# A list scheduler gets measured durations, and bursts on TensorE must wait for its instruction packets

## The chip, the cores and the metric

The kernel runs on one core of a Trainium2 chip. The metric is the time of one execution on the device in microseconds (us). Five engines work side by side on a core, each through its own list of instructions in order: TensorE (PE, with its weight loads shown apart as PEld), VectorE (DVE), ScalarE (ACT), GpSimd (POOL) and SyncE (SP), which issues the DMA transfers. They meet only at semaphores.

## The reference, cut to what matters

Three stages follow each other on 4 x 768 = 3072 tokens of width 384:

```python
# attention with a decaying state, 8 heads of 48, for every step t:
y[t]  = r[t] @ (state + outer(u * k[t], v[t]))
state = w[t][:, None] * state + outer(k[t], v[t])
# first feed-forward, 384 -> 1536 -> 384
x = (sigmoid(x @ w_gate) * (x @ w_val)) @ w_out
# second feed-forward, 384 -> 2048 -> 384
h = x @ w_in
out = (h * tanh(softplus(h))) @ w_out2
```

All of it is float32.

## The kernel before, in words

**Tiling.** The 768 steps are cut into 24 chunks of 32, and two chunks make a pair: 12 pairs, numbered p = 0 to 11. A pair's 256 tokens go through attention and then, while the next pair's attention is under way, through the first feed-forward. The second feed-forward takes 512 tokens at a time once all pairs are through. A float32 matrix product is made of three float16 products (high by high, high by low, low by high), and the weights of all feed-forwards are decoded from 64-bit words into those halves on the chip, on ACT, DVE and POOL, until some 114 us (the first feed-forward's) and mostly from some 486 us on (the second's).

**Attention of a pair.** `fine(p)` multiplies and sums small blocks (POOL, DVE), `coarse(p)` turns operands on DVE, makes the scores on TensorE (`scores`, tile lp) and merges them (`merge`, tile X). `turn_keys` (pair 1 alone, tile kt) or `keys` bring the keys into place, `states_apart` (pairs 0 and 1) or `states` update the state (tile kp), and `rows_out` makes the output rows (tile yp). `turn` brings these rows into xt, through TensorE (tile xp) for pairs 0 and 1 and by a transposing DMA for the later ones.

**First feed-forward of a pair.** `gate(p, i)` makes 128 x 256 blocks of both products (tile gv). One call of its `fill` is nine matmuls with nine weight loads, 18 instructions; 24 fills belong to a pair. `out1` (tile o of the line L1201) is of the same size and shape. For these the weights have to be decoded, and for `gate` xt has to be there.

**Bursts.** The attention's matmuls are small and follow each other fast: lp, kt, kp and yp are one task each, of 129 to 385 instructions. They are called bursts and carry `burst=space(p)`: after one, no other burst is begun for 3.0 (pairs 0 and 1) or 5.0 planned us.

**Order.** Nothing is ordered by hand. Every piece of work is a `Task` with a planned cost on each engine that may do it, what it reads and writes, a `lat` (time after its end until others see it) and `words`, the number of its instructions on TensorE. `Plan.run` works out a due time for each (`late`), backward from the end. `Plan.schedule` then plays the plan forward in its own time: at each moment every free engine takes, of the tasks that are ready, the one with the earliest due time, on the engine where it is cheaper if two may do it. The order in which tasks are taken is the order in which each engine's instructions are written, so the planned costs decide the order and have no other effect: nothing on the chip waits for a planned time. While both DVE and POOL are busy with tasks that use the memory port they share (`port`), the plan lets them run at the shares in `SHARE` (L68). `COLD` = 1.9 (L37) is a factor on the cost of some early TensorE tasks, `BURST` = 1.42 that of a usual burst.

**Packets.** The plan takes TensorE's instructions to come in packets of `WORDS` = 256, with an offset of `ORIGIN` = 67, and counts them in `at_word`. `crowded` (L149) puts a burst of 208 words or more behind all other ready tasks if more than 208 of them lie within one packet. A burst that is put behind is still begun when TensorE has nothing else ready in the plan.

Of the kernel before, what the change touches and what calls it, by code (L numbers as in the profile page):

```python
# [48 lines left out]
COLD = 1.9  # L49
BURST = 1.42  # L50
# [2 lines left out]
TURNED = (1,)  # L53
KBANKS = ((('pg', 0), ('pg', 1)), (('at', 0), ('at', 2)))
ONE = 13
JOIN = 0.3
GATHER = 0.36
PARTS = ((), (0,), (1,), (2, 3))
SPACE = 3.0
# [3 lines left out]
WORDS = 256  # L63
MERGE = lambda p, e: e == 0
CROWD = 208
SWEEPS = 1
INF = float("inf")
SHARE = {"dve": 0.42, "pool": 0.72}  # L68
ENGS = ("pool", "dve")
W1HI = {"act": 0.83}  # L70
W1LO = {"dve": 0.92, "pool": 1.65}
# [11 lines left out]
class Plan:  # L83
# [57 lines left out]
            t.fn(e)  # L141

    def schedule(self, follow):
        now = rested = 0.0
        at_word = ORIGIN
        coming, busy, queues, order = [], {}, {}, []
        left = {t: len(t.deps) for t in self.tasks}

        def crowded(t):  # L149
            if t.words < CROWD:  # L150
                return False
            first = WORDS - at_word % WORDS
            return max(min(first, t.words), t.words - first) > CROWD

        def arrive(t):
            at = max([d.end + d.lat for d in t.deps], default=0.0)
            heapq.heappush(coming, (at, t.rank, t))

        def finish(t):
            t.end = now  # L160
            for n in follow[t]:
                left[n] -= 1
                if left[n] == 0:
                    arrive(n)

        def best(e):
            return min(
                (bool(t.burst) and (now < rested or crowded(t)), t.late, t.rank, t)
                for t in queues[e]
            )[1:]  # L170

        for t in self.tasks:
            if not t.deps:
                arrive(t)
        while len(order) < len(self.tasks) or busy:
            while True:
                while coming and coming[0][0] <= now + 1e-9:
                    t = heapq.heappop(coming)[2]
                    for e in t.cost:
                        queues.setdefault(e, []).append(t)  # L180
                picks = []
                for e in queues:
                    if queues[e] and e not in busy:
                        late, rank, t = best(e)
                        picks.append((late, rank, t.cost[e], e, t))
                if not picks:
                    break
                _, _, _, e, t = min(picks, key=lambda x: x[:3])
                for k in t.cost:
                    queues[k].remove(t)  # L190
                t.begin = now
                order.append((e, t))
                if e == "pe":
                    at_word += t.words
                if e == "none":
                    finish(t)
                else:
                    busy[e] = [t.cost[e], t]
                if t.burst:
                    rested = now + t.cost[e] + t.burst  # L200
            shared = all(e in busy and busy[e][1].port for e in SHARE)
            rate = {e: SHARE[e] if shared and e in SHARE else 1.0 for e in busy}
            step = min((busy[e][0] / rate[e] for e in busy), default=INF)
            if coming:
                step = min(step, coming[0][0] - now)
            now += step
            for e in list(busy):
                busy[e][0] -= step * rate[e]
                if busy[e][0] < 1e-9:
                    finish(busy.pop(e)[1])  # L210
        return order
# [3 lines left out]
def mixer_moe_kernel(  # L215
# [15 lines left out]
    add = plan.add  # L231
# [21 lines left out]
    A = fp.tile([128, 1184], F32, name="A")  # L253
# [6 lines left out]
    def attn(eng, cost, fn, reads=(), writes=(), lat=SEM, burst=0.0, words=18, port=False):  # L260
        add(eng, cost, fn, [*reads, "attention"], writes, lat, burst, words, port)

    def space(p):
        return SPACE if p < 2 else SPACED
# [25 lines left out]
    words = {}  # L290
# [38 lines left out]
    def decode(key, dst, n, count, slot, reads, high_on, lo_on, halves=False, blocks=None):  # L329

        raw = ("raw", slot)
        word = ("word", count % 2)
        low = ("low", count % 2)
        name = f"{key[0]}{key[1]}"

        def rebase(e):
            words[key] = dp.tile(
                [128, *n], F32, tag=f"word{count % 2}", name=f"word_{name}"  # L340
            )
            rebased(words[key], raws[key][:, :, :, 1])

        def bits3(e):
            lows[key] = dp.tile([128, *n], U32, tag=f"low{count % 2}", name=f"low_{name}")
            spare_bits(key)

        def join(e):
            bits = words[key].bitcast(U32)
            nc.vector.scalar_tensor_tensor(  # L350
                out=bits,
                in0=bits,
                scalar=3,
                in1=lows.pop(key),
                op0=ALU.logical_shift_left,
                op1=ALU.bitwise_or,
            )

        def high(e):
            put = nc.scalar.copy if e == "act" else nc.vector.tensor_copy  # L360
            put(out=dst()[:, 0], in_=words[key])

        def rest(e):
            engines[e].tensor_tensor(  # L364
                out=dst()[:, 1], in0=words.pop(key), in1=dst()[:, 0], op=ALU.subtract
            )

        add("act", 0.78, rebase, [raw, "consts", "table1"], [word])
        add("act", 1.1, bits3, [raw, "consts"], [low])
        add("dve", 0.85, join, [low], [word], port=True)  # L370
        if halves:
            combine(key, dst, word, low, reads, high_on, lo_on, count)
            return
        made = [[(key[0], f, a) for f in blocks or [key[1]]] for a in range(2)]
        add(high_on, 0, high, [word, *reads], made[0])
        add(lo_on, 0, rest, [word, *made[0]], made[1])
# [40 lines left out]
    def decode_early(name, i, dst, src, count):  # L417

        slot = count % 3
        raw = ("raw", slot)  # L420
        low = ("low", count % 2)
# [4 lines left out]
            lows[key] = dp.tile([128, KC, 256], U32, tag=f"low{count % 2}", name=f"low_{name}{i}")  # L426
            spare_bits(key)

        add("act", 1.1, bits3, [raw, "consts"], [low])
        for h in range(2):  # L430
            f = 2 * i + h
            hs = slice(128 * h, 128 * h + 128)
# [28 lines left out]
                    op=ALU.subtract,  # L461
                )

            add("act", 0.43, rebase, [raw, "table1"], [bank])
            add("dve", 0.48, join, [low], [bank])
            add("act", 0.39, high, [bank], [(name, f, 0)])
            add("dve", 0.47, rest, [bank, (name, f, 0)], [(name, f, 1)])

# [33 lines left out]
    def load_pair(p):  # L504
        edges = (0, C * DH, C * (DH + DP), BLK)

        def new(e):
            blk[p] = fp.tile([128, BLK], F32, tag=f"blk{p % 2}", name=f"blk{p}")

        def go(e, i):  # L510
            if i is None:
                new(e)
            cs = slice(0, BLK) if i is None else slice(edges[i], edges[i + 1])
            nc.sync.dma_start(out=blk[p][:, cs], in_=rkw[p, :, cs])

        keys = [("blk", p % 2, i) for i in range(3)]
        if p == 1:
            attn("sp", 3.6, lambda e: go(e, None), [], keys, lat=2.0)
            return

        after = [[], [("x2d", p - 4, KC - 1)], [("x2d", p - 3, 0)]]
        attn("none", 0, new, [], keys, lat=0.0)
        for i in range(3):
            late[p, i] = lambda i=i: attn(
                "sp", 1.2, lambda e: go(e, i), after[i] if p > 3 else [], [keys[i]], lat=2.0
            )
            if p <= 3 or i == 0:
                late.pop((p, i))()
# [19 lines left out]
    def fine(p):  # L548
# [3 lines left out]
        def products(mult, cost, shape, cell, scaled=False):  # L552
# [19 lines left out]
            if scaled:  # L572
                attn("dve", 0.95, times_u, ["U"], [pt], port=True)
            cells.append(("A", len(cells)))
            attn("dve", 0.86 if cost > 1 else 0.47, total, [pt, "A"], [cells[-1]])

        products(
            lambda e, pv, r, k: times(e, pv, r, k),
# [63 lines left out]
    def coarse(p, cells):  # L642
# [83 lines left out]
        attn(both, 0, lambda e: scaled(e, 5, 6, 1, 4), [WD], [(*RD, 2)])  # L726
        attn({"dve": 0.6, "pool": 1.05}, 0, lambda e: scaled(e, 2, 4, 2, 2), [WD, (*RD, 2)], [(*RD, 1)])
        parts = [(*RD, n) for n in range(3)]
        attn("pe", BURST, scores, [*parts, KD], [*banks, ("lp", p)], burst=space(p), words=256)
        attn("dve", 1.9, flip_a, [*cells], X[0] + X[1])  # L730
        for e in range(2):
            for n in range(4):
# [212 lines left out]
    def states_apart(p, e):  # L945
# [27 lines left out]
            for hf in range(2):  # L973
                decay(p, e, hf)
        parts = [("KK", p % 2, q, g, h) for q in range(4) for g in range(2) for h in range(2)]
        attn("pe", 1.17 * COLD, sums, [*parts, ("v", j % 3)], banks, burst=space(p), words=129)
        for hf in range(2):
            both = {"dve": 0.48} if j else {"act": 0.5, "dve": 0.48}
            attn(both, 0, lambda on, hf=hf: put(on, hf), [banks[hf]], S(j + 1)[2 * hf : 2 * hf + 2])
# [1 line left out]
    def rows_out(p, es, banks):  # L981
# [36 lines left out]
                                    stop=(n == 1 or j == 0),  # L1018
                                )

        cost = 2.58 if len(es) > 1 else BURST * (COLD if p < 2 else 1.0)
        attn("pe", cost, sums, [*X, *RD, *V, *old], banks, burst=space(p), words=257 if p else 193)
        xs = [[("xs", e, t, i) for i in range(2) for e in es] for t in range(2)]

# [91 lines left out]
    def gate(p, i):  # L1116
# [55 lines left out]

        def fill(o, h):
            w = [(("wg", "wv")[o], two[h], a) for a in range(2)]
            cold = COLD if p == 0 and two[h] < 3 else 1.0
            add("pe", 0.99 * cold, lambda e: sums(o, h), [*x, *w, "gates"], [banks[o]])

        def finish():
# [521 lines left out]
```

## Time and profile before

| | |
|---|---|
| time, median of 3 runs | 920.1 us (919.99 to 920.99) |
| span of the profiled execution | 917.8 us |
| what lies around the span | 2.3 us of the median |
| TensorE busy in the span | 866.2 us, 94% |
| VectorE, ScalarE, GpSimd busy | 633.6, 490.7, 506.4 us |
| instruction packets | queue q8: 102, 1.67 MB |

The profile is of one execution. A busy share is of the whole span, and stages with different limits lie in it, so the span is read stretch by stretch. Matmuls overlap, so the time of one is longer than the distance to the next. "Idle before" is time in which an engine stood still just before an instruction, with what ended it; "issue" there is time in which the engine waited for nothing that the profile shows. The granted clock of TensorE (PEclk) is 1.00 at 2.4 GHz and 0.50 at 1.2 GHz.

### The profile page before, as it was taken

How to read it: one execution, taken by the hardware profiler on the slowest of the kernel's cores; microseconds unless marked ns; L12 is line 12 of the kernel's file. 1: busy time of each engine (PE TensorE's matmuls, PEld its weight loads, DVE VectorE, ACT ScalarE, POOL GpSimd, SP SyncE). 2: the span in 40 equal slices, each digit the busy share in tenths (PEclk: the TensorE clock that was granted, in tenths of full speed). 3: DMA queues.
4: the chain of work that ended last, by engine and by line, in shares of the span. 5: the costliest groups of instructions: out<-in, count | busy, mean ns of one | idle time of the engine just before them, and what ended most of it. 6: DMA issues, size and time to landing. Idle time of an engine off the chain costs nothing.

```text
span 917.8 us, 29861 instructions
## 1 busy us (share of the span) xinstructions
PE 866.2 (94%) x13064; PEld 701.3 (76%) x13064; DVE 633.6 (69%) x1098; ACT 490.7 (53%) x1125; POOL 506.4 (55%) x562
## 2 busy tenths in 40 slices
PE   0578899999999999999999999999999999999998
PEld 0456788888888888888888885577677676776788
DVE  7897898877585777767688768765655655556541
ACT  2687854363543525262548777764655655556540
POOL 7996976646557474847553476543533434335320
PEclk9998999999999999999999999999999999999999
DMA  9277633222322232332306910100101002000001
GB/s 333 88 240 250 226 102 101 69 71 71 99 84 60 80 87 75 69 91 54 79 23 189 260 47 13 43 5 10 61 1 46 25 1 70 1 27 10 2 35 36
DMA packets 55315, 74.29 MB, mean 81 GB/s; under 512 B 19600, under 2 KB 36496, under 8 KB 55056
## 3 DMA queue, kind: packets, MB, share of 16 engines
q1 hardware_dynamic: 55184, 72.38, 26.3%
q8 instruction: 102, 1.67, 0.8%
q14 instruction: 29, 0.24, 0.1%
HBM read 58.99 MB, written 9.44 MB: 75 GB/s over the span
## 4 chain that ended last, share of the span: by engine, by line
PE 85%; POOL 4%; DVE 4%; ACT 3%; DMA 2%; issue 1%; SPq 0%; DVEq 0%; ACTq 0%; POOLq 0%
PE gv L1133 27%; PE h L1311 20%; PE o L1426 18%; PE o L1201 14%; PE yp L1013 3%; POOL pt L546 2%; PE kp L910 2%; POOL blk L546 1%; ACT KK L851 1%; ACT X L716 1%; PE lp L695 1%; POOL wos L364 1%; DMA raw_wv<-wv 1%; DVE A L566 1%; PE kt L806 0%
## 5 line engine op out<-in xcount | busy, mean ns | idle before, releaser
L1311 PE MATMUL h<-x,wis 128*128 128x512 f16 x864 | 199.9, 379 | 0.0
L1345 POOL TENSOR_TENSOR sum<-e 128x256 f32<-128x256 f32 x96 | 71.9, 748 | 179.9 <-ACT e L1322 179.9
L1133 PE MATMUL gv<-xt,wgs 128*128 128x256 f16 x1296 | 166.5, 274 | 4.8 <-DVE gt L1164 3.1
L1133 PE MATMUL gv<-xt,wvs 128*128 128x256 f16 x1296 | 165.6, 275 | 2.1 <-ACT sig L1144 1.8
L1201 PE MATMUL o<-gt,wos 128*128 128x256 f16 x1296 | 163.5, 273 | 0.0
L1311 PEld LDWEIGHTS <-wis 128*128 128x128 f16 x864 | 83.5, 98 | 82.9
L1133 PEld LDWEIGHTS <-wgs 128*128 128x128 f16 x1296 | 125.5, 98 | 21.7 <-issue 4.7
L1133 PEld LDWEIGHTS <-wvs 128*128 128x128 f16 x1296 | 126.4, 99 | 19.3 <-issue 2.2
L546 POOL TENSOR_TENSOR blk<-blk 128x384 f32<-128x384 f32 (+4 forms) x151 | 123.2, 829 | 30.1 <-DMA blk<-rkw 11.9
L1201 PEld LDWEIGHTS <-wos 128*128 128x128 f16 x1296 | 125.8, 98 | 17.9 <-issue 0.2
L546 POOL TENSOR_TENSOR pt<-blk 128x384 f32<-128x384 f32 x93 | 105.6, 1160 | 35.8 <-DMA blk<-rkw 33.1
L1322 ACT ACTIVATE e<-h 128x512 f32<-128x512 f32 x96 | 57.3, 597 | 85.9 <-PE h L1311 84.9
L1149 DVE SCALAR_TENSOR_TENSOR gv<-gv,sig 128x512 f32<-128x512 f32 x72 | 50.6, 703 | 54.2 <-ACT sig L1144 26.2
L1144 ACT ACTIVATE sig<-gv 128x512 f32<-128x512 f32 x72 | 42.1, 596 | 81.8 <-PE gv L1133 81.5
L1161 ACT CAST gt<-gv 128x512 f16<-128x512 f32 x72 | 42.2, 585 | 67.7 <-DVE gv L1149 67.5
L1426 PE MATMUL o<-wps,gt 128*128 128x192 f16 x612 | 74.0, 246 | 0.0
L887 POOL TENSOR_TENSOR s<-s,WD 128x384 f32<-128x384 f32 x40 | 37.1, 936 | 55.6 <-DVE s L939 35.7
L851 ACT COPY KK<-KT 32x192 f32<-32x192 f32 (+1 forms) x168 | 59.9, 357 | 10.9 <-DVE KT L836 8.5
L1364 DVE SCALAR_TENSOR_TENSOR gt<-e,gt 128x256 f16<-128x256 f32 x41 | 27.5, 683 | 49.6 <-ACT gt L1359 49.6
L1426 PE MATMUL o<-wps,wgs 128*128 128x192 f16 x498 | 59.4, 246 | 0.0
L1164 DVE TENSOR_TENSOR gt<-gv,gt 128x512 f16<-128x512 f32 x72 | 49.3, 685 | 13.2 <-ACT gt L1161 12.9
L1426 PE MATMUL o<-wps,wos 128*128 128x192 f16 x456 | 57.1, 246 | 0.0
(123 smaller groups left out, 1461.8 us busy)
## 6 DMA issues: line engine op xcount, KB each, us to landing
v<-vt SPq DMA_DIRECT2D x24, 480.0 KB, 4.1
blk<-rkw SPq DMA_DIRECT2D x22, 384.0 KB, 3.6
raw_wi<-wi SPq DMA_DIRECT2D x8, 768.0 KB, 5.7
raw_wp<-wo SPq DMA_DIRECT2D x8, 768.0 KB, 5.6
blk<-rkw SPq DMA_DIRECT2D x11, 512.0 KB, 4.3
raw_wg<-wg SPq DMA_DIRECT2D x6, 768.0 KB, 5.4
raw_wv<-wv SPq DMA_DIRECT2D x6, 768.0 KB, 5.4
raw_wo<-wo SPq DMA_DIRECT2D x6, 768.0 KB, 5.2
```

The costliest lines, as they stand in the source:

```text
L546: engines[e].tensor_tensor(out=pv, in0=a, in1=b, op=ALU.mult)
L851: nc.scalar.copy(out=to, in_=own)
L1133: nc.tensor.matmul(gps[p, i, o][:, h], w[:, a, kc, fs], xt[p][:, c, kc, :], start=(n == 0), stop=(n == 3 * KC - 1),)
L1144: nc.scalar.activation(out=sgs[p, i], in_=gps[p, i, 0], func=AF.Sigmoid, scale=1.0 / (SW * SX))
L1149: nc.vector.scalar_tensor_tensor(out=gps[p, i, 1], in0=gps[p, i, 1], scalar=SG / (SW * SX), in1=sgs.pop((p, i)), op0=ALU.mult, op1=ALU.mult,)
L1161: nc.scalar.copy(out=gt[p][:, 0, 2 * i : 2 * i + 2], in_=gps[p, i, 1])
L1164: nc.vector.tensor_tensor(out=gt[p][:, 1, 2 * i : 2 * i + 2], in0=gps[p, i, 1], in1=gt[p][:, 0, 2 * i : 2 * i + 2], op=ALU.subtract,)
L1201: nc.tensor.matmul(ops[p, c][:, :NT], wos[:, a, f, cs], gt[p][:, g, f, :], start=(f == 0 and n == 0), stop=(f == NF1 - 1 and n == 2),)
L1311: nc.tensor.matmul(hps[r, f], w2["wi"][:, a, kc, fs], x2[r][:, c, kc, :], start=(n == 0), stop=(n == 3 * KC - 1),)
L1322: nc.scalar.activation(out=es[r, f], in_=hps[r, f], func=AF.Mish, scale=ih)
L1345: engines[e].tensor_tensor(out=sums[0][:, n - 1], in0=a(), in1=b(), op=op)
L1426: nc.tensor.matmul(ops2[h, first], home(slots[r, i, name])[:, c, tsl], w2["wp"][:, a, w, i, :], start=(new and n == 0), stop=(n == 3 * NF2 ...
```

## The change

Two things are changed, both in the plan. No instruction is added or taken away; tasks are the same, and so are their dependencies.

**Durations.** Planned costs of decoding steps, sums, merges of the state, four early TensorE tasks, the shares of DVE and POOL and one transfer latency get other values.

**A condition for bursts.** When a task on TensorE reaches the end of a packet, the plan notes `ready`: the moment at which the end is reached plus `FETCH` = 3.2. A burst that would reach the next end before `ready`, by its planned cost, counts as unfit, as crowded bursts and those within the spacing do. The rest of the diff in `schedule` is the same selection with heaps in place of a scan.

```diff
-JOIN = 0.3
+JOIN = 0.32
+FETCH = 3.2
-SHARE = {"dve": 0.42, "pool": 0.72}
+SHARE = {"dve": 0.58, "pool": 0.78}
...
-        def crowded(t):
-            if t.words < CROWD:
-                return False
+        def unfit(t):
+            if now < rested:
+                return True
             first = WORDS - at_word % WORDS
-            return max(min(first, t.words), t.words - first) > CROWD
+            if t.words > first and now + t.cost["pe"] * first / t.words < ready:
+                return True
+            return t.words >= CROWD and max(min(first, t.words), t.words - first) > CROWD
...
         def best(e):
-            return min(
-                (bool(t.burst) and (now < rested or crowded(t)), t.late, t.rank, t)
-                for t in queues[e]
-            )[1:]
+            queue, bursts = queues[e]
+            while queue and queue[0][2] in taken:
+                pop(queue)
+            if not bursts:
+                return queue[0] if queue else None
+            found = min((unfit(t), late, rank, t) for late, rank, t in bursts)
+            if queue:
+                found = min(found, (False, *queue[0]))
+            return found[1:]
...
                 if e == "pe":
+                    first = WORDS - at_word % WORDS
+                    if t.words >= first:
+                        ready = now + t.cost[e] * first / t.words + FETCH
                     at_word += t.words
...
-        add("act", 0.78, rebase, [raw, "consts", "table1"], [word])
-        add("act", 1.1, bits3, [raw, "consts"], [low])
-        add("dve", 0.85, join, [low], [word], port=True)
+        add("act", 0.91, rebase, [raw, "consts", "table1"], [word])
+        add("act", 1.0, bits3, [raw, "consts"], [low])
+        add("dve", 0.96, join, [low], [word], port=True)
-        add("act", 1.1, bits3, [raw, "consts"], [low])
+        add("act", 1.0, bits3, [raw, "consts"], [low])
-            add("act", 0.43, rebase, [raw, "table1"], [bank])
-            add("dve", 0.48, join, [low], [bank])
-            add("act", 0.39, high, [bank], [(name, f, 0)])
-            add("dve", 0.47, rest, [bank, (name, f, 0)], [(name, f, 1)])
+            add("act", 0.5, rebase, [raw, "table1"], [bank])
+            add("dve", 0.52, join, [low], [bank])
+            add("act", 0.46, high, [bank], [(name, f, 0)])
+            add("dve", 0.51, rest, [bank, (name, f, 0)], [(name, f, 1)])
...
-                "sp", 1.2, lambda e: go(e, i), after[i] if p > 3 else [], [keys[i]], lat=2.0
+                "sp",
+                1.2,
+                lambda e: go(e, i),
+                after[i] if p > 3 else [],
+                [keys[i]],
+                lat=2.0 if p else 3.2,
...
-            attn("dve", 0.86 if cost > 1 else 0.47, total, [pt, "A"], [cells[-1]])
+            attn("dve", 0.9 if cost > 1 else 0.5, total, [pt, "A"], [cells[-1]])
...
-        attn("pe", BURST, scores, [*parts, KD], [*banks, ("lp", p)], burst=space(p), words=256)
+        attn("pe", BURST if p else 1.75, scores, [*parts, KD], [*banks, ("lp", p)], burst=space(p), words=256)
...
-        attn("pe", 1.17 * COLD, sums, [*parts, ("v", j % 3)], banks, burst=space(p), words=129)
+        attn("pe", 1.17 * (1.0 if j else COLD), sums, [*parts, ("v", j % 3)], banks, burst=space(p), words=129)
...
-        cost = 2.58 if len(es) > 1 else BURST * (COLD if p < 2 else 1.0)
+        cost = (2.58 if p else 3.4) if len(es) > 1 else BURST * (COLD if p < 2 else 1.0)
...
-            cold = COLD if p == 0 and two[h] < 3 else 1.0
+            cold = COLD if p == 0 and two[h] < 1 else 1.0
```

## Rows read from the trace of the kernel before

**Rows 1.** The page, TensorE's busy time over the whole span.
```profile
PE 866.2 (94%) x13064; PEld 701.3 (76%) x13064; DVE 633.6 (69%) x1098; ACT 490.7 (53%) x1125; POOL 506.4 (55%) x562
```

**Rows 2.** Busy time by stretch: stretch and length, PE, PEld, DVE, ACT, POOL, PEclk, DMA.
```profile
0.00:25.60 25.60, 0.00 (x0) 0.00 (x0) 17.72 (x22) 5.19 (x7) 18.82 (x26) 1.00 0.87 314
25.60:43.80 18.20, 11.34 (x460) 9.02 (x460) 16.34 (x24) 12.15 (x29) 17.81 (x17) 1.00 0.23 75
43.80:66.10 22.30, 18.87 (x319) 15.00 (x318) 22.30 (x33) 18.97 (x35) 20.57 (x20) 1.00 0.73 234
66.10:98.70 32.60, 23.41 (x682) 19.42 (x680) 26.54 (x46) 26.08 (x47) 23.25 (x22) 0.90 0.67 234
98.70:149.70 51.00, 47.78 (x1006) 41.71 (x1005) 45.61 (x69) 28.12 (x61) 39.96 (x36) 1.00 0.50 148
150.00:550.00 400.00, 399.92 (x7616) 354.60 (x7615) 294.57 (x505) 201.27 (x486) 236.22 (x250) 1.00 0.33 89
550.00:914.00 364.00, 364.00 (x2983) 260.90 (x2982) 209.82 (x404) 198.75 (x464) 149.75 (x195) 1.00 0.07 23
```

**Rows 3.** Waits of PE: who waited for whom, us in total, times, longest.
```profile
PE xp L1065 <- DVE xs L1044: 3.8, 2, 2.2
PE yp L1013 <- issue: 3.2, 1, 3.2
...
...
PE gv L1133 <- DMA xt<-xs: 1.4, 1, 1.4
```

**Rows 4.** PE in order of time, around pair 1's bursts: start, length, work.
```profile
69.19 4.51 PE L806 MATMUL kt<-first,blk 128*32 128x32 f32 x192 [2.82 <-ACT X L716]
...
75.61 1.15 PE L1133 MATMUL gv<-xt,wvs 128*128 128x256 f16 x9
76.69 0.31 PE L1013 MATMUL yp<-v,X 64*32 64x48 f32 x15
...
81.18 0.29 PE L1013 MATMUL yp<-s,RD 64*32 64x48 f32 x9 [3.20 <-issue]
...
82.72 3.47 PE L1133 MATMUL gv<-xt,wvs 128*128 128x256 f16 x18
...
98.66 1.16 PE L1133 MATMUL gv<-xt,wgs 128*128 128x256 f16 x9
```

**Rows 5.** PE in order of time, the same fills later.
```profile
115.40 2.13 PE L1133 MATMUL gv<-xt,wvs 128*128 128x256 f16 x18
```

**Rows 6.** Busy time and counts up to and within the stop in yp, columns as in Rows 2.
```profile
0.00:75.60 75.60, 36.89 (x988) 30.20 (x989) 64.56 (x91) 45.57 (x90) 66.62 (x68) 0.98 0.61 208
0.00:79.00 79.00, 39.27 (x1116) 32.17 (x1117) 67.73 (x100) 48.09 (x94) 69.94 (x72) 0.98 0.63 216
77.90:81.10 3.20, 0.08 (x9) 0.00 (x0) 2.75 (x4) 1.36 (x2) 3.12 (x5) 1.00 1.04 412
82.10:85.40 3.30, 3.30 (x18) 2.38 (x16) 1.46 (x4) 3.25 (x6) 0.00 (x0) 0.50 0.61 195
```

**Rows 7.** DMA queues: packets, MB, share of 16 engines.
```profile
q8 instruction: 102, 1.67, 0.8%
```

**Rows 8.** DVE in order of time, its wait for pair 1's xp.
```profile
86.57 0.56 DVE L1071 COPY xt<-xp 128x768 f16<-128x768 f16 x1 [3.01 <-PE xp L1065]
```

**Rows 9.** Groups of instructions by line and shape: busy us, mean ns, idle before.
```profile
L306 ACT ACTIVATE word_wv<-raw_wv 128x768 f32<-128x768 f32 x6 | 5.6, 941 | 0.0
```

**Rows 10.** DVE in order of time, the join of a tile beside busy and idle POOL.
```profile
35.38 1.79 DVE L350 SCALAR_TENSOR_TENSOR word_wv<-word_wv,low_wv 128x768 uint32<-128x768 uint32 x1
...
87.04 0.95 DVE L350 SCALAR_TENSOR_TENSOR word_wv<-word_wv,low_wv 128x768 uint32<-128x768 uint32 x1
```

**Rows 11.** POOL in order of time, its idle stretch and the state's decay.
```profile
88.93 1.65 POOL L364 TENSOR_TENSOR wvs<-word_wv,wvs 128x768 f16<-128x768 f32 x1 [7.00 <-ACT wvs L361]
91.94 0.83 POOL L887 TENSOR_TENSOR s<-s,WD 128x384 f32<-128x384 f32 x1 [1.36 <-DVE s L967]
...
94.34 1.54 POOL L887 TENSOR_TENSOR s<-s,WD 128x384 f32<-128x384 f32 x1
```

More of the change, by code (lines that the diff above doesn't have):

```diff
@@ L143, in schedule @@
     def schedule(self, follow):
-        now = rested = 0.0
+        now = rested = ready = 0.0
         at_word = ORIGIN
@@ L147, in schedule @@
         left = {t: len(t.deps) for t in self.tasks}
-        def crowded(t):
-            if t.words < CROWD:
-                return False
+        taken = set()
+        push, pop = heapq.heappush, heapq.heappop
+        def unfit(t):
+            if now < rested:
+                return True
             first = WORDS - at_word % WORDS
-            return max(min(first, t.words), t.words - first) > CROWD
+            if t.words > first and now + t.cost["pe"] * first / t.words < ready:
+                return True
+            return t.words >= CROWD and max(min(first, t.words), t.words - first) > CROWD
         def arrive(t):
             at = max([d.end + d.lat for d in t.deps], default=0.0)
-            heapq.heappush(coming, (at, t.rank, t))
+            push(coming, (at, t.rank, t))
         def finish(t):
@@ L177, in schedule @@
                 while coming and coming[0][0] <= now + 1e-9:
-                    t = heapq.heappop(coming)[2]
+                    t = pop(coming)[2]
                     for e in t.cost:
-                        queues.setdefault(e, []).append(t)
+                        queue, bursts = queues.setdefault(e, ([], []))
+                        if t.burst:
+                            bursts.append((t.late, t.rank, t))
+                        else:
+                            push(queue, (t.late, t.rank, t))
                 picks = []
                 for e in queues:
-                    if queues[e] and e not in busy:
-                        late, rank, t = best(e)
-                        picks.append((late, rank, t.cost[e], e, t))
+                    if e not in busy:
+                        found = best(e)
+                        if found:
+                            late, rank, t = found
+                            picks.append((late, rank, t.cost[e], e, t))
                 if not picks:
@@ L188, in schedule @@
                 _, _, _, e, t = min(picks, key=lambda x: x[:3])
-                for k in t.cost:
-                    queues[k].remove(t)
+                taken.add(t)
+                if t.burst:
+                    queues[e][1].remove((t.late, t.rank, t))
                 t.begin = now
```

## The prediction, made before the changed kernel ran

> **What bounds the kernel now.** I read four views: the page's busy times, busy time by stretch, TensorE's waits, TensorE's list in time. On the page TensorE is busy 866.2 of 917.8 us [rows 1], so 51.6 us are idle. The stretches say where: none of them lies late. From 150 to 550 us TensorE is busy 399.92 of 400.00, from 550 to 914 all of 364.00 [rows 2]. In these stretches a new order can only exchange work with work, at no gain. The idle time is before 149.7 us: 25.6 us until the first matmul, then 18.20 - 11.34 = 6.9, 22.30 - 18.87 = 3.4, 32.60 - 23.41 = 9.2 and 51.00 - 47.78 = 3.2 [rows 2], 22.7 in sum. Whatever the change does to the time, it does there: by the moment at which TensorE gets into its full stretch.
>
> What ends the waits there? Between 43.8 and 66.1 us DVE is busy 22.30 of 22.30 us [rows 2]: TensorE waits for vector work that nothing can hurry. From 66.1 to 98.7 all three vector engines have room: DVE 6.1, ACT 6.5, POOL 9.3 us [rows 2]. This is the stretch to look at. It ends with pair 1's first gv at 98.66 [rows 4], and TensorE's only other work in it, pair 0's fills, is short: 24 fills at 2.13 / 2 = 1.07 each [rows 5] are some 26 us, from 43.8 on. So fills are padding here, and the chain that counts is pair 1's attention: lp, kt, yp, kp, yp, kp, and through xp to xt.
>
> In that chain stand a 2.82 us wait of kt for ACT's merges, and a stop of 3.20 us in the middle of a yp burst, ended by "issue", with no semaphore named (both in [rows 4]). The counts explain it. TensorE has 13064 matmuls and as many loads [rows 1], 26128 instructions in the 102 transfers of queue q8 [rows 7], 256 each. With the plan's offset of 67 the packets end at 189 + 256 n. At 79.00 us, in the stop, 1116 + 1117 = 2233 have begun; 189 + 8 x 256 = 2237 [rows 6]. The packet before ended at 1981, and 988 + 989 = 1977 had begun at 75.60 [rows 6]. So TensorE crossed one end at about 75.6, needed the next packet at about 77.9, and went on at 81.18, 5.6 us after the crossing [rows 4]. In the stop the DMA engines are full: share 1.04, 412 GB/s [rows 6]. I take the packet to stand behind the loads of weights and of the next blocks; the rows show both at once, not the cause.
>
> The stop has a second price. From 82.10 to 85.40 the granted clock is 0.50, 1.2 GHz [rows 6], after TensorE had stood still; 18 gv matmuls take 3.47 us there and 2.13 at full clock [rows 4, 5], 1.3 more. And others wait behind: DVE 3.01 us for xp, POOL 7.00 for a cast [rows 8, 11].
>
> The Trainium skill, "Runtime: NRT & Kernel Launch", section "Instruction fetch mechanics", has blocks of 256 instructions, fetched by the sequencer while it runs the one before, at a cost it calls "mostly hidden", since instructions are dispatched more slowly than blocks arrive. By that the condition on bursts has nothing to save. The block size agrees with the counts above; on the cost this trace agrees for nearly all of the 102 packets, and differs by 3.20 us at one.
>
> **The change, part by part.** No instruction is added or removed, and all waits are the same dependencies; only places in each engine's list move. So no engine's busy time changes, except by the clock and by who runs beside whom.
>
> *The condition on bursts.* What it can save is the stop and the slow clock, 3.20 + 1.34 = 4.5 us. Would it catch this burst? If the order up to there stayed, hardly. The plan prices yp of pair 1 at 1.42 x 1.9 = 2.70 for 257 instructions; the burst began at about instruction 1995 (2233 less 119 matmuls and their loads), 242 before the end, so the plan has it reach that end 2.54 after its begin. It began about 1.0 after the crossing [rows 4, 6]; crossing plus 3.2 is 2.2 after the begin, and 2.54 is later. The condition lets it pass, by 0.3. On the chip the burst gets there in 1.2, and the packet came 4.6 after the begin. Moreover only the first end in a task is noted, and kt with its 385 instructions can cross two. So the condition helps only together with the shifted order: one or two fills fewer or more between kt and yp move the end out of the burst or the crossing away from it. Of the 256 possible offsets I count those as bad in which a crossing in or after kt is followed by another in yp within 5.6 us: with 384 + 54 + 256 = 694 instructions from kt to the end of yp, about 180 of 256, but those with the first crossing early in kt cost little, as 4 to 5 us pass. A stop over 1.5 us, with the first crossing 128 to 182 into kt, comes in 54 of 256, a fifth. Being put behind costs too, as the bursts are the chain: a fill is 1.07 [rows 5], one or two fills 1.5. Net 4.5 - 1.5 = 3.0 where the stop goes.
>
> *Durations of ACT and DVE.* The plan had rebase at 0.78, the trace has 0.941 [rows 9]; the new 0.91 is close. The join of a tile takes 0.95 beside an idle POOL and 1.79 beside a busy one [rows 10], a share of 0.53: the old plan had 0.85 / 0.42 = 2.02 there, the new one 0.96 / 0.58 = 1.66. POOL's share moves away from the trace: its decay takes 0.83 alone and 1.54 beside DVE's join [rows 11], 0.54, and the plan goes from 0.72 to 0.78. No row tells what order follows. The bounds: at best the new order uses the room of DVE in the two stretches after 66.1, 6.1 + 5.4 us [rows 2], of which the stop holds about 3 already, so some 8 gained; at worst it opens waits of the size of those for xp and of kt again, 3.8 + 2.8 [rows 3, 4], some 6 lost. I take 0, with a good half of the chance on the better side, since two of three are nearer to the rows.
>
> *TensorE's early costs* (cold factors off four fills and three kp bursts, 1.75 and 3.4 for pair 0) and *pair 0's latency*. TensorE is not the limit until 43.8, as DVE and POOL are busy 17.7 and 18.8 of the first 25.6 us and 16.3 and 17.8 of the next 18.2 [rows 2]. I take 0, with 2 us either way from the first 25.6, where the order of DVE and POOL can move.
>
> *After 150 us.* The condition puts bursts some fills later, and TensorE has fills enough: 0. If that cover went, it would show as idle time in the stretch of 399.92.
>
> **The sum.** 917.8 - 3.0 = 914.8 us of span; with the 2.3 us around it, 920.1 - 917.8, the forecast is 917.1 us.
>
> **The rivals.**
>
> *The gain is taken back at xt of pair 2, or the stop stays.* Pair 2's fills begin only after its xt, where TensorE now waits 1.4 us for the transfer [rows 3], ending at about 149.6. For it speaks that DVE is busy 45.61 of 51.00 us before it [rows 2]: if pair 2's chain is not earlier, 3.0 us saved at 98.7 are 3.0 us more wait there. The same time results if the burst passes the condition as worked out above. Against it: DVE's and POOL's idle 3.01 and 7.00 us behind the stop would shrink too. Time: 920.1, within 1 us. This time has two ways to it, the second of them small: that packets are on time in any order, and the stop in yp had another cause, such as the full DMA engines of [rows 6] holding up something that the trace does not show. Then the condition saves none of its 3.20 us, and only puts bursts behind. Its chance is 0.04 of the 0.25 below, as the stop falls within four instructions of a packet's end. The Trainium skill, "Runtime: NRT & Kernel Launch", section "Instruction fetch mechanics", has this rule.
>
> *Slower: the condition holds up pair 1's chain.* Six bursts stand between 62.5 and 98.7 us in a row, each may be put behind by up to 3.2 planned us, and fills are taken in their place, of which there is no lack until pair 0's are used up. It decides from two bursts put behind by two fills where no stop is saved: 2 x 2 x 1.07 = 4.3 us, less what overlaps with vector work: +4, 924. For it speaks that fills are padding up to 98.66; against, that most of these bursts wait for ACT or DVE anyway.
>
> *More: the new durations also take away kt's wait.* With merges and casts better placed on ACT, kt's 2.8 [rows 4] and half of xp's 3.8 [rows 3] go too: 3.0 + 2.8 + 1.9, about -8, 912.
>
> **How the numbers follow.** The forecast's case (-3, from -6 to -1) has 0.43, the gain of 8 has 0.10, no change 0.25, slower 0.22. Under 0.2%, 1.8 us, cannot be told from no change. Faster: 0.9 of the first, all of the second and little of the third, 0.50. Same: 0.26; slower: 0.24. The range leaves out a tenth at each side: 910 to 924.5; the likeliest case alone has 914 to 919.
>
> **What would show it.** Right: no "issue" wait over 1 us in yp or kp, a clock of 1.00 from 75 to 98 us, pair 1's first gv at about 95.5, and 150 to 550 us still full. Taken back: that gv earlier, but a longer wait for xt of pair 2. Wrong: a stop of 3 us at another packet's end, or pair 1's first gv after 100.

## The result, and the profile after

The changed kernel takes 924.39 us (median of 4 runs, 921.72 to 927.38) where the kernel before takes 920.05 in the same comparison: a ratio of 1.0055, 95% interval 1.0039 to 1.0071. It is slower by some 4 us; 3.0 us of gain were forecast. The profiled execution has a span of 919.9 us, the shortest of the four, 2.1 us longer than that of the kernel before; its rows show less of the loss than the medians do.

The page's row of TensorE and the busy time by stretch, of the changed kernel (columns as in [rows 2]):

```profile
PE 867.8 (94%) x13064; PEld 701.8 (76%) x13064; DVE 633.6 (69%) x1098; ACT 489.5 (53%) x1124; POOL 506.7 (55%) x563
```

```profile
25.60:43.80 18.20, 12.45 (x469) 9.97 (x470) 16.45 (x30) 15.57 (x36) 17.81 (x16) 1.00 0.34 110
43.80:66.10 22.30, 19.42 (x329) 15.49 (x327) 21.27 (x29) 17.41 (x32) 19.62 (x19) 1.00 0.78 266
66.10:98.70 32.60, 24.24 (x692) 20.54 (x692) 28.09 (x47) 27.13 (x48) 30.94 (x28) 0.90 0.68 228
98.70:149.70 51.00, 47.49 (x1000) 41.33 (x998) 46.39 (x73) 27.60 (x69) 38.53 (x36) 1.00 0.51 143
150.00:550.00 400.00, 397.27 (x7575) 351.13 (x7573) 293.37 (x498) 196.33 (x471) 232.58 (x248) 1.00 0.32 87
550.00:914.00 364.00, 364.00 (x2978) 260.63 (x2976) 208.02 (x401) 200.10 (x464) 148.29 (x194) 1.00 0.07 23
```

Against [rows 2], TensorE is busier in each of the first three stretches shown, by 1.1, 0.6 and 0.8 us. In the stretch from 150 to 550, which was full (399.92), it now stands still for 2.73 us. TensorE's waits in the same profile, to be read against [rows 3]:

```profile
PE kp L935 <- ACT KK L876: 2.5, 7, 0.4
PE gv L1158 <- DMA xt<-xs: 2.4, 2, 1.7
...
PE yp L1038 <- issue: 2.2, 2, 1.2
...
PE gv L1158 <- DVE X L741: 2.0, 1, 2.0
```

Two kinds of these reach into the late part. The gates wait for xt twice (1.7 us at pair 2, just before 150 us, and 0.7 at pair 3), and kp waits seven times for key copies on ACT, five of these times after 150 us, 1.85 us in sum. TensorE's list around pair 1's bursts, which answers to [rows 4]:

```profile
68.25 4.60 PE L831 MATMUL kt<-first,blk 128*32 128x32 f32 x192 [2.11 <-ACT X L741]
74.88 1.14 PE L1158 MATMUL gv<-xt,wgs 128*128 128x256 f16 x9 [2.03 <-DVE X L741]
...
81.12 0.23 PE L1038 MATMUL yp<-s,RD 64*32 64x48 f32 x2 [1.17 <-issue]
...
90.23 0.31 PE L1038 MATMUL yp<-s,RD 64*32 64x48 f32 x14 [1.08 <-issue]
...
93.73 2.30 PE L1226 MATMUL o<-gt,wos 128*128 128x256 f16 x9
...
97.37 1.16 PE L1158 MATMUL gv<-xt,wgs 128*128 128x256 f16 x9
```

Pair 1's first gv comes at 97.37, 1.29 us earlier, and 18 matmuls of out1, two fills or about 2 us, are done before it, where the kernel before had none: TensorE is 3.3 us further. I counted TensorE's matmuls of both traces in order, weighed by their kind, and compared the times at equal work. The changed kernel leads by 3.3 us between 128 and 141 us, by 2.6 once pair 2's gate runs, by 1.5 from 188 us on; it is level at 279, 1.3 behind at 363 and 2.1 behind from 547 us on. The early gain is there, and 5.4 us are lost later. Idle time is only part of that: of the 4.7 us lost after 150 us it holds 2.7, as a burst that is broken up also takes longer while TensorE counts as busy.

The steps of that loss are kp bursts and gate starts. Pair 7's kp, and the key copies on ACT before it, in the changed kernel (the kernel before in the two fences after them):

```profile
361.26 0.49 PE L935 MATMUL kp<-v,KK 32*64 32x48 f32 x10
362.17 0.32 PE L935 MATMUL kp<-v,KK 32*64 32x48 f32 x4 [0.41 <-ACT KK L876]
362.90 1.42 PE L935 MATMUL kp<-v,KK 32*64 32x48 f32 x114 [0.41 <-ACT KK L876]
```

```profile
358.86 3.98 ACT L876 COPY KK<-KT 32x192 f32<-32x192 f32 x11
```

```profile
361.21 1.84 PE L910 MATMUL kp<-v,KK 32*64 32x48 f32 x128
```

```profile
359.03 2.55 ACT L851 COPY KK<-KT 32x192 f32<-32x192 f32 x7
```

Before, the last copy ends at 361.58 and the burst runs through. After, copies run until 362.84, the burst is begun 1.6 us before that and follows them one by one: it takes 3.1 us in place of 1.8, of which 0.82 count as idle, and all fills behind it wait with it. The burst is begun at the same moment in both, 361.21 and 361.26; what is later is the vector work before it. DVE's transposition of the keys, and the first copies on ACT behind it, before and then after:

```profile
350.37 2.09 DVE L836 STREAM_TRANSPOSE KT<-blk 128x768 f32<-128x768 f32 x1
352.50 3.24 ACT L851 COPY KK<-KT 32x192 f32<-32x192 f32 x9 [1.73 <-DVE KT L836]
```

```profile
351.51 2.10 DVE L861 STREAM_TRANSPOSE KT<-blk 128x768 f32<-128x768 f32 x1
353.64 1.80 ACT L876 COPY KK<-KT 32x192 f32<-32x192 f32 x5 [2.82 <-DVE KT L861]
```

In the changed order DVE takes a product of the first feed-forward (gt) and a sum (xo) ahead of the transposition, which it took behind it before. So the copies begin 1.1 us later, five of the sixteen instead of nine are done when ACT turns to its twelve merges of X, and eleven are left for the end.

### The profile page after: what moved, and what is told of

Same layout as the page of the kernel before. It is cut to its first block, busy times and chain, and to the rows that moved or that the text cites. A ratio compares the mean times of both kernels' runs of the same rounds, so it can differ in the third digit from the quotient of the medians.

```text
span 919.9 us, 29869 instructions
## 1 busy us (share of the span) xinstructions
PE 867.8 (94%) x13064; PEld 701.8 (76%) x13064; DVE 633.6 (69%) x1098; ACT 489.5 (53%) x1124; POOL 506.7 (55%) x563
## 4 chain that ended last, share of the span: by engine, by line
PE 77%; DVE 7%; ACT 7%; POOL 3%; DMA 3%; issue 2%; SPq 0%; DVEq 0%; POOLq 0%; ACTq 0%
PE gv L1158 22%; PE h L1336 20%; PE o L1451 18%; PE o L1226 11%; PE yp L1038 3%; ACT KK L876 3%; DMA xt<-xs 2%; ACT X L741 2%; PE kp L935 2%; DVE A L591 1%; DVE KT L861 1%; PE lp L720 1%; POOL blk L571 1%; POOL sum_wp L409 1%; DMA raw_wp<-wo 1%
## 5 line engine op out<-in xcount | busy, mean ns | idle before, releaser
L571 POOL TENSOR_TENSOR blk<-blk 128x384 f32<-128x384 f32 (+4 forms) x150 | 126.0, 852 | 32.9 <-DMA blk<-rkw 18.3
L703 POOL TENSOR_TENSOR RD<-RD,WD 128x768 f32<-128x768 f32 (+2 forms) x34 | 37.2, 1094 | 36.7 <-PE lp L720 32.5
```

Source lines behind the costliest of these rows:

```text
L571: engines[e].tensor_tensor(out=pv, in0=a, in1=b, op=ALU.mult)
```

## The experiments

Each was compared with the kernel before on the same chip; ratios are to it, with 95% intervals.

**1. Without the condition on bursts.** With this value the noted moment `ready` never lies ahead, so no burst is unfit by it.

```diff
-FETCH = 3.2
+FETCH = -1e6
```

> The changed kernel with the condition on bursts switched off (FETCH far below zero). In the plan the condition turns out never to decide: with it off, the order of every engine is instruction for instruction that of the changed kernel (and the kernel before with the condition added keeps its order too). So this is the changed program again, and the whole change lies in the durations. Theory: the same time as the changed kernel, 922 to 927 us, ratio to before 1.002 to 1.008, and the same two places of loss: waits of kp bursts for the key copies after 150 us, some 2.5 us in all. What it tells besides: whether the executions of one program spread by some us (921.7 to 927.4 so far) because of different waits, by the span, the clock and the profile of another execution. Rival: if the condition did anything on the chip, this run would differ from the changed kernel by over 3 us.

Measured: 925.92 us, 1.0076 [1.0064, 1.0089]. Its instructions stand on every engine in the very order of the changed kernel: at 3.2 us the condition never changes which task is taken, and on the costs of before it moves nothing either. It is without effect; what is left of the change is its durations and shares. The two comparisons of this one order, 1.0055 and 1.0076, say 0.4 to 0.9% slower. Their profiled executions differ by 4.2 us of span, and these rows show one place of it, pair 5's kp and the fills after it, here and then in the changed kernel:

```profile
277.60:281.60 4.00, 3.17 (x138) 2.52 (x136) 3.10 (x5) 3.87 (x11) 0.00 (x0) 1.00 0.02 4
281.60:285.00 3.40, 3.40 (x19) 2.42 (x17) 2.34 (x8) 0.29 (x1) 1.66 (x2) 0.50 0.56 151
```

```profile
280.60:284.00 3.40, 3.40 (x34) 3.05 (x32) 2.86 (x9) 0.34 (x1) 1.66 (x2) 1.00 0.58 152
```

The same two waits of 0.41 us in the same burst are followed here by 3.4 us at 1.2 GHz, in which 19 matmuls are done and not 34; there the clock stays. So one such stop costs the 1.3 us by which the burst is longer, or that and the work of 15 fill matmuls, some 1.6 us more. Pair 7's kp, with the same two waits, is followed by 0.50 here too, from 366.9 us on, and not there. Twice 1.6 us, and 1.2 us more at pair 3's gate (which waits 1.93 us for xt here and 0.72 there), come to about the 4.2.

**2 and 3. Durations alone, shares alone.**

```diff
-SHARE = {"dve": 0.58, "pool": 0.78}
+SHARE = {"dve": 0.42, "pool": 0.72}
```

> The new durations with the old shares of DVE and POOL (0.42 and 0.72); the condition is there and without effect. Theory A (the new shares make the plan too hopeful for the vector engines, so that kp bursts stand in TensorE's list where their key copies are ready in the plan and not on the chip): with the old, pessimistic shares no waits of kp for key copies over 0.3 us after 150 us, TensorE busy at least 399.5 of 400 us from 150 to 550; but the early gain of 3.3 us at 145 us goes too, and the time is 918 to 924. Rival B (the durations of ACT and DVE do it): the waits of kp stay at 2 us or more here.

Measured: 930.18 us, 1.0119 [1.0106, 1.0132].

Shares alone is the kernel before with one line changed, the reverse of the line above.

> The kernel before with the new shares alone (0.58 and 0.78); its durations are the old ones. Theory A: the shares bring both the early gain and the late loss: TensorE some 2 to 5 us ahead of the kernel before at 145 us, and at least 1.5 us idle from 150 to 550 us, most of it in kp bursts that wait for ACT's key copies; time 917 to 924. Rival B: the shares alone leave 150 to 550 us full (399.5 or more busy).

Measured: 926.92 us, 1.0083 [1.0066, 1.0100]. Either half is slower than before, and the whole is not their sum. Neither theory fits either of them: TensorE is busy 394.64 and 395.01 of 400 us from 150 to 550, but only 0.8 and 0.9 us of the idle time are kp waiting for key copies. The stop of a packet is also back, with the new shares on the order of the old durations:

```profile
78.89 0.30 PE L1013 MATMUL yp<-s,RD 64*32 64x48 f32 x10 [4.06 <-issue]
```

**4. Key copies planned 2 us later, from pair 2 on**, so that the plan puts kp behind more fills.

```diff
...
-            at = max([d.end + d.lat for d in t.deps], default=0.0)
+            at = max([d.end + d.lat + d.slack for d in t.deps], default=0.0)
...
-                    attn("act", cost, lambda e, a=(g, q, h, n): gather(*a), ["KT"], kk)
+                    attn("act", cost, lambda e, a=(g, q, h, n): gather(*a), ["KT"], kk, slack=2.0 if p >= 2 else 0.0)
```

> The changed kernel with one thing added: from pair 2 on, the plan takes the key copies on ACT to be ready 2.0 us later than it did (in the forward play alone, not in the due times). TensorE's order is that of the changed kernel up to its 64th task, about 121 us. Theory A: the waits of kp for key copies go, TensorE is busy 399 of 400 us or more from 150 to 550, and the time falls by 2.5 to 4.5 us against the changed kernel, to about 919 to 921 as the median (917 in the best execution), at or below the kernel before. Rival C (from pair 3 on the attention's chain sets the pace, since its transposed keys come at the same moments in both kernels, 269.4 and 269.7, 310.6 and 310.7 us; TensorE's early lead can only be waited away): the idle time moves to another place and the time stays within 1 us of the changed kernel.

Measured: 929.89 us, 1.0121 [1.0107, 1.0136]. The cure works and the gain does not come, so the theory that the new costs are merely too hopeful for the key copies falls: kp waits for no copy any more, but the stretch and the waits show the idle time elsewhere, and more of it.

```profile
150.00:550.00 400.00, 391.14 (x7523) 345.43 (x7523) 296.17 (x493) 187.60 (x457) 225.28 (x241) 1.00 0.32 88
```

```profile
PE gv L1159 <- ACT sig L1170: 6.1, 6, 1.9
PE gv L1159 <- DVE gt L1190: 4.6, 4, 1.8
PE yp L1039 <- issue: 3.6, 3, 1.9
PE gv L1159 <- DMA xt<-xs: 3.2, 2, 1.8
```

**5. New shares until 140 planned us, the old ones from there.**

```diff
+LATER = {"dve": 0.42, "pool": 0.72}
...
-            rate = {e: SHARE[e] if shared and e in SHARE else 1.0 for e in busy}
+            share = SHARE if now < 140 else LATER
+            rate = {e: share[e] if shared and e in share else 1.0 for e in busy}
```

> The changed kernel, whose plan uses the new shares of DVE and POOL only up to 140 planned us and the old ones (0.42, 0.72) after. Every engine's order is that of the changed kernel up to 147 planned us. Theory A (after 150 us the plan is too hopeful because of the new shares, and this alone brings the waits there): the lead of 3.0 to 3.3 us over the kernel before at the work of 85 us stays, TensorE is busy 399 of 400 us or more from 150 to 550, and the median falls to 917 to 921. Theory D (the kernel before stands on a picked order; any other order, however its costs were changed, has waits of 4 to 10 us more on the chip): new waits from 150 to 550 of 3 us or more, median 922 to 930.

Measured: 927.28 us, 1.0090 [1.0071, 1.0109]. The lead at 145 us is there and is lost again, with TensorE busy 393.05 of 400 us from 150 to 550. The shares are not what is wrong in the late part either.

**6 and 7. The kernel before, with one cost moved by about 1%.** No reason speaks for either value; they only make the plan come out otherwise.

```diff
-SHARE = {"dve": 0.42, "pool": 0.72}
+SHARE = {"dve": 0.425, "pool": 0.72}
```

> The kernel before with DVE's share at 0.425 in place of 0.42, and nothing else: no cost comes nearer to a measured one by anything that matters. The orders part at 51 to 84 planned us. Theory D (picked order): the time rises by 3 to 10 us, to 923 to 930, with waits in the middle stretch that the kernel before has not. Theory A, or any theory by which the size or the direction of the cost changes decides: within 1.5 us of the kernel before.

Measured: 925.75 us, 1.0088 [1.0059, 1.0117].

```diff
-GATHER = 0.36
+GATHER = 0.362
```

> The kernel before with the planned cost of a key copy at 0.362 in place of 0.36, and nothing else. The orders part at 125 planned us, so all before stays, the stop in yp at 77.8 us too. Theory D: 2 to 8 us slower, all of it after 125 us. Theory A: within 1.5 us of the kernel before.

Measured: 929.71 us, 1.0115 [1.0096, 1.0135]. These moves mean nothing and cost as much as the whole change or more. The stretch in each, in this order:

```profile
150.00:550.00 400.00, 397.11 (x7583) 351.49 (x7581) 293.16 (x504) 198.59 (x480) 234.55 (x249) 1.00 0.33 90
```

```profile
150.00:550.00 400.00, 394.95 (x7549) 348.90 (x7549) 286.57 (x491) 190.85 (x462) 223.97 (x240) 1.00 0.32 88
```

**8. The kernel before, with the condition alone and at 5.0 us**, where it does act. It is written as the changed kernel with all durations and shares taken back (left out here) and this line:

```diff
-FETCH = 3.2
+FETCH = 5.0
```

> The kernel before with the condition on bursts at 5.0 us in place of 3.2, the first round value at which it decides anything before 280 planned us; all durations are the old ones. The orders part at 63 planned us. By the forecast's reckoning the stop of 3.2 us in pair 1's yp and the half clock after it go: at the work of 40 us TensorE is 2 to 4.5 us ahead of the kernel before, and if nothing else happens the time is 916 to 918. Theory D: that lead is there at the work of 40 us, and is given back by waits after it; 920 to 928.

Measured: 927.40 us, 1.0091 [1.0069, 1.0113]. The lead that was expected under either theory is not there. At equal work TensorE is some 3 us behind the kernel before at 145 us, after a wait of kp for xt of 3.5 us, and from 150 to 550 us it is busy 395.22 of 400. So a condition that acts did not bring the forecast's gain. The burst of pair 1 still meets a packet's end:

```profile
81.00 0.39 PE L1038 MATMUL yp<-s,RD 64*32 64x48 f32 x9 [2.64 <-issue]
```

**9 to 12. Spliced orders.** Up to here the theory was that the early part of the changed order is good and its late part bad. These kernels test it by parts. The order is no longer planned but written out: tasks that one plan begins before a cut stand as there, all others in the order and on the engines of the other plan.

```diff
...
-        for e, t in self.schedule(follow):
-            t.fn(e)
+        for x in TAKE.split():
+            self.tasks[int(x[1:])].fn(names[x[0]])
...
```

> The order is spliced: what the changed plan begins in its first 138 us (up to before gate of pair 2) stands as in the changed kernel, everything else in the order and on the engines of the kernel before. Nothing is left out. Theory D (the early gain of 3 us is real, the loss is in the new order of pairs 2 to 11): the lead of 3.0 to 3.3 us at 145 us is there, the rest has hardly an idle moment, 916 to 917.5 where the kernel before shows 919 to 920. Rival E (the lead cannot be kept in any order, as transfers, ACT and DVE keep their own pace behind it): the gate of pair 2 and later bursts wait until the 3 us are gone, 919 to 921. Rival F (any order not picked on the chip is worse, the splice too, since 25 tasks that were begun earlier are missing from the later order): waits of a few tenths to 2 us in 150 to 550, 923 or more.

Measured: 916.41 us, 0.9966 [0.9953, 0.9979].

> The reverse splice: what the plan of the kernel before begins in its first 138 us stands as there, everything else in the order of the changed kernel. Nothing is left out. Theory D (the loss of 5 to 8 us lies in the new order of pairs 2 to 11 by itself): no lead at 145 us, and the stops of kp for key copies as in the changed kernel, 924 to 928. Rival E (the lead makes its own loss, as TensorE runs up against engines that keep their pace): without the lead there are no such stops, kp waits under 0.5 us in sum, and the time is that of the kernel before within 1.5 us.

Measured: 928.92 us, 1.0103 [1.0087, 1.0119].

> As the first splice, but the changed order is kept only for what its plan begins in the first 100 us (through pair 1's attention), and the order of before follows from there. Theory D: the lead is already 4 to 5 us after pair 1's attention, and 2 to 3 of it are left at 145 us; 916 to 918. Rival E: gone by pair 3, 919 to 921. Rival F: 923 or more. If this one gains and the first does not, the join at 138 us costs it; if both gain, the early part of the changed order is worth its 3 us.

Measured: 914.73 us, 0.9951 [0.9936, 0.9967], faster than both kernels.

> As the splices before, but the changed order stands only for what its plan begins in the first 60 us, that is up to about where pair 1's bursts begin; the order of before follows from there. Nothing is left out. Theory G (the lead comes from the vector work before pair 1's bursts, placed better by the new durations; the traces have TensorE 3 to 4 us ahead at about 60 us already, before the stop in yp): a lead of 3 us or more after pair 0, kept to the end, 915 to 917.5. Theory H (the lead comes from pair 1's bursts standing otherwise to the ends of the instruction packets, as was forecast): most of the lead is gone at the bursts of pair 1, as these have the order of before again, 918.5 to 920.5.

Measured: 919.38 us, 0.9996 [0.9986, 1.0007].

The reverse splice lies a little above what was expected of it, the third splice below. The two stretches that decide, of the first, second and third splice:

```profile
98.70:149.70 51.00, 47.79 (x1007) 41.94 (x1005) 44.45 (x66) 25.21 (x60) 37.74 (x36) 1.00 0.48 144
150.00:550.00 400.00, 399.92 (x7603) 353.16 (x7601) 297.29 (x508) 202.62 (x488) 236.24 (x253) 1.00 0.32 87
```

```profile
98.70:149.70 51.00, 47.44 (x1003) 41.62 (x1001) 47.45 (x70) 28.45 (x66) 40.60 (x37) 1.00 0.51 144
150.00:550.00 400.00, 395.68 (x7561) 350.15 (x7561) 292.87 (x503) 196.67 (x477) 231.00 (x245) 1.00 0.32 88
```

```profile
98.70:149.70 51.00, 50.02 (x1030) 44.08 (x1028) 47.58 (x75) 28.16 (x69) 37.96 (x35) 1.00 0.49 141
150.00:550.00 400.00, 399.92 (x7592) 352.12 (x7590) 296.45 (x504) 202.42 (x484) 239.27 (x255) 1.00 0.32 87
```

With the late order of before the stretch from 150 to 550 is full again, although TensorE comes 3.4 or 6.6 us earlier (first and third). So engines that keep their own pace do not eat the lead, as rival E had it, nor is every order that was not picked on the chip worse by itself, as rival F had it. With the late order of the changed kernel it is not full, without any lead to run ahead with. The second splice has the stops of the changed kernel at the same bursts, with five copies ahead of the merges and eleven behind them as there; pair 7's kp:

```profile
366.46 0.49 PE L1121 MATMUL kp<-v,KK 32*64 32x48 f32 x10
367.36 0.32 PE L1121 MATMUL kp<-v,KK 32*64 32x48 f32 x4 [0.41 <-ACT KK L1062]
368.10 1.42 PE L1121 MATMUL kp<-v,KK 32*64 32x48 f32 x114 [0.41 <-ACT KK L1062]
```

In microseconds by the ratios the early part of the changed order is worth 3.1 (1.9 to 4.3) and the late part costs 9.5 (8.0 to 11), 6.4 in sum; the two comparisons of the whole say 5.1 and 7.0. The parts add up.

The first matmul of the second feed-forward shows where each stands, and that nothing differs behind it. Operation, count, duration in ns, first and last start, of before, of after and of the three splices in turn:

```profile
L1311 PE MATMUL h<-x,wis x864: 379/379/379, 549.8 to 884.5; 128*128 128x512 f16 x173
```

```profile
L1336 PE MATMUL h<-x,wis x864: 379/379/379, 551.9 to 886.6; 128*128 128x512 f16 x173
```

```profile
L1522 PE MATMUL h<-x,wis x864: 379/379/379, 546.3 to 880.9; 128*128 128x512 f16 x173
```

```profile
L1522 PE MATMUL h<-x,wis x864: 379/379/379, 556.5 to 891.2; 128*128 128x512 f16 x173
```

```profile
L1522 PE MATMUL h<-x,wis x864: 379/379/379, 543.1 to 877.8; 128*128 128x512 f16 x173
```

From first to last it is 334.6 or 334.7 us in all five. In the profiled executions the third splice is 3.2 us ahead of the first. Some 1.5 of that are pair 2's gate, which waits for xt no longer, where the first still waits 1.35 us and the kernel before 1.4 [rows 3]; the other 1.7 come between 95 and 123 us, by work done, where the order of before stands better behind the cut. In the medians it is 1.7.

The fourth splice leaves the source of the early gain half settled. In its profiled execution TensorE leads by some 3 us at 60 us, which speaks for the vector work before pair 1's bursts (theory G). But at the next burst lp waits 2.05 us for DVE's sums of the state (s), which neither of the two kernels does, and the granted clock is at 0.50 around it:

```profile
61.70:71.90 10.20, 7.25 (x291) 6.24 (x293) 7.89 (x14) 6.65 (x19) 9.19 (x10) 0.50 0.07 14
```

```profile
63.00 1.72 PE L906 MATMUL lp<-RD,KD 64*32 64x48 f32 x120 [2.05 <-DVE s L1178]
...
80.29 0.29 PE L1224 MATMUL yp<-s,RD 64*32 64x48 f32 x10 [3.19 <-issue]
```

When kt begins, 0.8 us of the lead are left (68.41 in place of 69.19). The stop in yp is back at its old size, as theory H expected, but it is not where the lead goes. This execution still ends 2.3 us ahead of the kernel before (spans of 915.5 and 917.8); it is one of the three fastest of twelve, and in the median nothing is left. So the gain also needs something of what the changed plan begins between 60 and 100 planned us: pair 1's bursts, and the vector work and fills beside them. Which of these carries it was not taken apart.

## Why the prediction was wrong

**What failed: the late part at nothing.** The step is "After 150 us. The condition puts bursts some fills later, and TensorE has fills enough: 0." Its basis was the reading of [rows 2] that in the full stretches "a new order can only exchange work with work". 399.92 of 400.00 is not a property of the work but of that one order, in which each kp, lp and gate happens to stand just behind what it needs. Fills give cover only where they stand ahead of the waiting burst in TensorE's list; behind it they wait too. And it was not the condition but the new durations that moved the late part, on DVE and ACT as well as on TensorE: pair 7's keys are transposed 1.1 us later, and kp stands at its old moment. The reverse splice puts the term at +9.5 us (8.0 to 11). The text named the sign to look for, idle time in that stretch, and gave it no price and hardly a chance.

**The durations at 0, bounded by 6 us of loss.** The bound came from two early waits. The late stretch has ten more pairs with some five joints each, and a bound would have had to count those. That two of three durations moved nearer to the rows was taken as half a reason for a gain. The runs give that no support: the durations without the shares cost 1.2%, the shares without the durations 0.8%, and values moved for no reason at all 0.9 and 1.2%.

**The early term: right size by luck, other cause.** Forecast 3.0, measured 3.1 by the first splice (and 4.5 by the third, which keeps less of the new order). But the condition on bursts, which was to bring it, changes no instruction's place. The prediction had worked out that this burst passes by 0.3 us, and then hoped for the shifted order. Nor do the stops go: TensorE stops 1.17 and 1.08 us in two yp bursts, and 2.03 us ahead of a gv at 74.88. The profile puts this last stop down to DVE X, but those merges run on until 75.37, and the count says otherwise. In the changed kernel, up to within that stop (columns as in [rows 2]):

```profile
0.00:74.00 74.00, 36.51 (x988) 30.02 (x989) 64.05 (x94) 45.36 (x90) 64.09 (x66) 0.98 0.66 227
```

988 + 989 = 1977 instructions have begun, four short of the packet's end at 1981, just as 2233 were four short of 2237 in the stop of the kernel before. That is 4.3 us in sum where the kernel before had 3.20, and the clock is at 0.50 for as long (mean 0.90 in both). "No issue wait over 1 us" and a gv at 95.5 were both wrong. By the profile, what gained were out1's fills, ready early enough to stand in the gaps between pair 1's bursts, and 1.3 us of earlier chain; no run moved these alone.

**The rivals.** "Taken back at xt of pair 2" is part of it: 0.7 us of the lead went there, 1.1 more at pair 3's gate. The slower rival has the time, 924, with a mechanism that did not occur, as the condition put no burst behind. No rival had the mechanism that decided.

**What stays open.** Why the plan's late orders come out so differently on the chip is followed back to its source at one joint, pair 7's kp; elsewhere it is shown in single waits, and it is not explained as a whole. The kernel before is the only planned order here whose stretch is full. That it was picked by time is an inference from how little it takes to lose it, not shown.

## What to carry to other kernels

A full engine under a fixed order is evidence about that order alone: when a change may reorder the stretch, price the joints where a small burst stands close behind its inputs, follow such a wait back through the other engines' lists, and move a cost by 1% to see how much any reordering is worth before crediting a reason. Where early and late parts of two orders differ, splice them by hand: here that showed a gain of 3 and a loss of 9 us that the whole had shown as one loss of 4 to 7, and gave a kernel 0.5% faster than either. Better planned durations need not make a better order.

## What the runs showed of the hardware

Two waits of 0.41 us within a burst, which hold TensorE up for 1.3 us, were followed by 3.4 us at 1.2 GHz in one execution, at two pairs, and by none in another of the same order (experiment 1). Bursts of small float32 matmuls met stops without a semaphore of 1.08 to 4.06 us in five of the orders shown here. Over all the kernels of this document, the profile has 20 stops of over 0.8 us in yp bursts that are ended by "issue". By the count of matmuls and weight loads begun, with packets ending at 189 + 256 n, each stands two to six instructions before a packet's end. The stop of 2.0 to 2.2 us after instruction 1977 is found in seven kernels, and the profile puts it down to DVE or ACT instructions. A new order moved and resized the stops, and a condition of 5.0 us in the plan left one of 2.64.
